# Own rows of V in four column groups, the other rows batched over eight segments

## The chip, the cores and the metric

The program runs on one core of a Trainium2 chip. The metric is the time of one execution on the device in microseconds, lower is better. One execution is profiled; its engines are called PE (TensorE, matrix products), PEld (its weight loads), DVE (VectorE), ACT (ScalarE), POOL (GpSimd) and SP (SyncE, which here only issues DMAs).

## What is computed

A transformer layer with a recurrent memory, and all its gradients. The input x has 2048 rows of 448 numbers, all in bf16. The attention goes over 64 segments of 32 rows, one after the other, with 16 heads of 256:

```
h = concat(mem, xs)                  # 8 memory rows and the 32 rows of the segment
q, k, v = h Wq, h Wk, h Wv           # 40 rows x 4096 each
p = softmax(mask(q k^T / 16))        # 40 x 40 for each head
o = (p v) Wo
mem = o[0:8]                         # memory of the next segment
out = o[8:40]
```

The layer then is `h = x + A(layernorm(x))` and `h2 = h + B(layernorm(h))`, where B is the gated network `(silu(x Wg) * (x Wu)) Wd` with 1792 hidden numbers. The kernel returns h2 and the gradients of nine inputs for a given gradient of the output. Because `mem` comes out of one segment and goes into the next, the 64 segments of the forward attention cannot run side by side, nor can those of the backward attention.

## The kernel before

Four parts follow one another: `forward_chain` (the 64 segments of the attention), `ffn_phase` (B, forward and backward), `backward_chain` (the 64 segments in reverse) and `tail_phase` (the gradients of the weights, large matrix products). Tiles lie in three arenas named arW (weights), arA and arB; PSUM has a pool of five banks `psf`, two banks `fx` and one bank `po`. A tile framework puts the instructions of each engine in order and sets the waits. What stands in `k.prio.crit()` comes first; `tc.issue_after(x)` puts an instruction behind x on x's engine. The code is unrolled.

The 40 rows of a segment are kept turned (features on partitions, `hT_roll`), the 32 rows of x in columns 0 to 31 and the memory in columns 32 to 39. The first 8 rows of x in each segment are called the rest rows here: columns 8 to 39, the other 24 rows and the memory, are the own rows. The rest rows don't depend on the recurrence. Q and K already use this: for the rest rows they are formed for eight segments at once, 64 rows in all (`rest_half`, L506), one unit of four chunks in each segment, in time for the next eight; `rest_rows` (L521) copies 8 rows of them into a segment's `qT_b` and `kT_b` on GpSimd. Units are done in segments 3 to 7 (two, two, two, one, one) for the second batch, and one in each of the segments 8 to 55. Segments 0 to 2 and 56 to 63 have none.

One segment runs like this in the program's lines:

- `qk_rows` (L590, L597): Q and K of the 32 own rows, four products of 32 columns side by side in the array; evicted, then turned by `qk_turned` (L614).
- `scores` (L698) in two halves of the heads; the mask is put into the bank first (L687). Heads come in two groups g: partitions 0 to 39 hold the queries of eight heads, partitions 64 to 103 those of the other eight.
- `shifted` and `softmax` for each half (L705 maximum, L706 subtraction, L707 exponential on ScalarE, L713 sum, L715 reciprocal, L716 product into `P_sb` in bf16).
- `value_rows` (L725) and `value_rest` (L733): V of all 40 rows, 64 stationary columns at a time (24 of them are not used), two products side by side, into four banks pV[0] to pV[3]; `value_out` evicts them into `Vs`, three on ScalarE and one on VectorE.
- `transposed_p` (L744): P turned with the identity, one matmul for each head and group (two banks `fx`), and evicted by VectorE and ScalarE into the block diagonal tile `PT_bd`.
- `values` (L757): P V for each half with 128 rows contracted, evicted into `xblk` (own rows) and `orr`.
- `out_proj` (L772), after which the sum of two halves is formed (L825 on ScalarE, L826 on VectorE). L832 turns the memory rows, L834 and L838 (GpSimd) put them into the next segment's `hT_roll`.

Behind this, each segment stores P (L843), Q and K (L845), V (L847) and the output rows (L841, L842) for later. Every 16 segments the output rows of the rest rows are formed for 16 segments at once (L876, 32 matmuls, into one `fx` bank); they are mixed into the segments that follow. The evictions all have the line of one helper: L75 on VectorE, L76 on ScalarE.

`backward_chain` reads P, Q, K and V back: `load_p` and `load_qk` (L1220, L1224), `load_v`.

## Time and profile before

| | us |
|---|---|
| median of 3 runs | 2878.65 (2863.39 to 2879.43) |
| profiled execution, its time | 2871.71 |
| profiled execution, its span | 2869.9 |
| forward chain, first L590 to the last L826 | 42.5 to 942.9 |
| one segment in the middle of it (L590 at 425.97 to L590 at 439.37) | 13.40 |
| busy in that segment: PE, DVE, ACT, POOL | 13.09, 7.52, 7.00, 4.44 |

The granted clock of TensorE is 0.988 in the mean. The span is the time from the first to the last instruction in the trace. A line of the timeline gives the start, the busy time, the engine, the line, the operation, what it writes and reads, and how often; a matmul's busy time overlaps that of the next, so the distance between starts says more about it than its length. In the chain of waits each piece has its start, its length, and what was worked on or waited for.

### The profile page before, as it was taken

The page shows a single profiled execution, that of the slowest core. Times are in us where ns is not written, and L with a number is a line of the kernel's source. Part 1 is how long each engine was busy: PE and PEld are TensorE (multiplying, and loading weights), DVE is VectorE, ACT ScalarE, POOL GpSimd, SP SyncE. Part 2 cuts the span into 40 slices and gives each one's busy share as a digit, 9 for nine tenths or more (in the row PEclk, how much of TensorE's full clock was granted, in tenths as well). Part 3 has the DMA queues.
Part 4 walks back from the last instruction along what each step waited for, and adds up shares of the span by engine and source line. Part 5 has one row for each costly group of instructions (what it writes and reads, how often), then busy time and mean ns, then how long its engine had stood idle before and what let it go on. Part 6 is the DMA issues. An engine that isn't in the chain of part 4 may idle for free.

```text
span 2869.9 us, 98023 instructions
## 1 busy us (share of the span) xinstructions
PE 2727.5 (95%) x41651; PEld 1575.5 (55%) x41651; DVE 1308.1 (46%) x3352; ACT 1046.2 (36%) x2579; POOL 929.0 (32%) x2065
## 2 busy tenths in 40 slices
PE   5999999999999999989999999999999989999998
PEld 3565555556555666645555555555655444445444
DVE  4555556465555677745555555555553111111110
ACT  2554455455454554433333433333332010111110
POOL 1222232232222232423454445545543211121211
PEclk9999999999999999989999999999999999999999
DMA  8577767777868999996777777777778998969951
GB/s 263 148 188 199 198 185 194 197 192 190 214 177 207 305 220 237 236 289 144 172 184 173 185 167 185 183 174 183 184 169 249 339 244 178 216 165 235 196 154 49
DMA packets 781806, 571.55 MB, mean 199 GB/s; under 512 B 632432, under 2 KB 673688, under 8 KB 778808
## 3 DMA queue, kind: packets, MB, share of 16 engines
q1 hardware_dynamic: 717080, 406.86, 60.7%
q0 software_dynamic: 64288, 158.41, 17.4%
q8 instruction: 328, 5.37, 0.8%
q14 instruction: 110, 0.90, 0.1%
HBM read 181.58 MB, written 244.92 MB: 149 GB/s over the span
## 4 chain that ended last, share of the span: by engine, by line
PE 73%; DMA 10%; issue 8%; ACT 3%; DVE 3%; POOL 2%; SPq 1%; POOLq 0%; ACTq 0%; DVEq 0%
PE bank L1334 9%; PE psf L1684 8%; PE psf L590 6%; PE psf L988 5%; PE psf L725 4%; PE bank L1181 4%; PE po L772 4%; PE fx L1684 3%; PE bank L1299 2%; PE fx L1113 2%; PE psf L614 2%; DMA arA<-VG 2%; PE bank L1354 2%; PE bank L1440 2%; PE psf L506 1%
## 5 line engine op out<-in xcount | busy, mean ns | idle before, releaser
L75 DVE CAST arA<-psf 128x512 bf16<-128x512 f32 (+2 forms) x285 | 159.9, 561 | 486.9 <-PE psf L1684 249.9
L76 ACT CAST arA<-psf 128x512 bf16<-128x512 f32 (+3 forms) x379 | 189.7, 509 | 523.9 <-PE psf L1684 215.2
L1334 PE MATMUL bank<-arW,arA 128*32 128x448 bf16 x6144 | 320.7, 357 | 4.9 <-DMA arW<-Tq 4.5
L76 ACT CAST arA<-bank 128x96 bf16<-128x96 f32 (+4 forms) x608 | 193.4, 376 | 111.7 <-PE bank L1322 95.5
L1684 PEld LDWEIGHTS <-arA 128*128 128x128 bf16 x1440 | 139.5, 99 | 161.9 <-issue 7.1
L1334 PEld LDWEIGHTS <-arA 128*32 128x32 bf16 x6144 | 155.8, 97 | 125.9 <-ACT arA L76 12.1
L1684 PE MATMUL psf<-arW,arA 128*128 128x512 bf16 x882 | 224.0, 383 | 0.0
L725 PE MATMUL psf<-arW,arA 128*64 128x512 bf16 x1536 | 212.2, 382 | 0.0
L590 PE MATMUL psf<-arW,arA 128*32 128x512 bf16 x3072 | 189.8, 381 | 7.8 <-DVE arA L75 0.9
L988 PE MATMUL psf<-arW 128*128 128x256 bf16 (+1 forms) x1288 | 146.1, 274 | 1.6 <-ACT arW L76 1.6
L1761 POOL DMA_DIRECT2D out_dram<-arA x96 | 51.9, 542 | 263.2 <-DVE arA L75 234.9
L1211 POOL DMA_DIRECT2D arA<-P_all x256 | 127.6, 504 | 23.1 <-issue 20.5
L75 DVE CAST arA<-bank 128x256 bf16<-128x256 f32 (+4 forms) x386 | 129.6, 391 | 6.4 <-PE bank L1181 4.1
L988 PEld LDWEIGHTS <-arW 128*128 128x128 bf16 (+1 forms) x1344 | 102.2, 97 | 51.6 <-issue 40.9
L772 PE MATMUL po<-arW,arA 128*32 128x256 bf16 (+1 forms) x4096 | 128.3, 262 | 1.7 <-DVE arA L75 1.2
L1181 PE MATMUL bank<-arW,arA 112*32 112x512 bf16 x2048 | 128.1, 392 | 1.6 <-DVE arA L1550 1.6
L590 PEld LDWEIGHTS <-arA 128*32 128x32 bf16 x3072 | 70.3, 96 | 105.2 <-issue 28.5
L1724 PE MATMUL psf<-arW 128*128 128x448 bf16 x525 | 112.8, 356 | 7.1 <-DVE arA L75 7.1
L772 PEld LDWEIGHTS <-arA 128*32 128x32 bf16 x4096 | 104.6, 96 | 9.6 <-DVE arA L75 1.5
L76 ACT CAST arB<-psf 128x64 bf16<-128x64 f32 (+1 forms) x192 | 65.1, 341 | 98.6 <-PE psf L597 76.3
L1227 POOL COPY arB<-arB 40x320 bf16<-40x320 bf16 x128 | 63.8, 498 | 114.7 <-DMA arB<-P_all 79.8
L725 PEld LDWEIGHTS <-arA 128*64 128x64 bf16 x1536 | 68.4, 109 | 52.8 <-issue 26.3
(321 smaller groups left out, 5101.0 us busy)
## 6 DMA issues: line engine op xcount, KB each, us to landing
arW<-T SPq DMA_DIRECT2D x256, 128.0 KB
X_o<-arA SPq DMA_DIRECT2D x37, 512.0 KB
T<-arA SPq DMA_DIRECT2D x64, 256.0 KB
X_v<-arA POOLq DMA_DIRECT2D x30, 512.0 KB
X_k<-arA POOLq DMA_DIRECT2D x30, 512.0 KB
X_q<-arA POOLq DMA_DIRECT2D x30, 512.0 KB
out_dram<-arA POOLq DMA_DIRECT2D x84, 128.0 KB
VG<-arA SPq DMA_DIRECT2D x64, 160.0 KB
```

Source lines behind the costliest of these rows:

```text
L75: return nc.vector.tensor_copy(out=out, in_=in_)
L76: return nc.scalar.copy(out=out, in_=in_)
L590: nc.tensor.matmul(banks[b][w][32 * q:32 * q + 32, :], lhsT=hT_roll[:, kc, sl, M:L], rhs=(Wq_sb, Wk_sb)[w][:, kc, col(q, b)], start=(b == ...
L725: nc.tensor.matmul(pV[b][64 * g:64 * g + 64, 0:512], lhsT=hT_flat[:, kc, sl * L:sl * L + 64], rhs=Wv_sb[:, kc, n * 512:(n + 1) * 512], sta ...
L772: last = nc.tensor.matmul(pO[32 * q:32 * q + 32, 0:w], lhsT=xblk[:, j, r * SEG:(r + 1) * SEG], rhs=Wo_sb[:, cj(j), 256 * dh:256 * dh + w], ...
L988: nc.tensor.matmul(ps[fp][:, f2 * 256:(f2 + 1) * 256], lhsT=Wt[lo:hi, kc, c * P:(c + 1) * P], rhs=xT[lo:hi, kc, :], start=(kc == 0 and f2 ...
L1181: last = nc.tensor.matmul(bank[32 * q:32 * q + 32, :], lhsT=lhs(c), rhs=WoT_sb[0:DQ, c, n0:n0 + 512], start=(c == 0), stop=(c == 3), skip_ ...
L1211: nc.gpsimd.dma_start(out=P4[32 * q:32 * q + 32, 2 * x + g], in_=pa[64 * g + M:64 * g + L, x])
L1227: pool_op = nc.gpsimd.tensor_copy(out=P_bd[64 * g:64 * g + L, :, g, :], in_=P_sb[64 * g:64 * g + L, :, :])
L1334: last = nc.tensor.matmul(ps[32 * q:32 * q + 32, 0:D], lhsT=lhs(j), rhs=WT[:, cj(j), :], start=(start and i < 4), stop=(stop and i >= len( ...
L1684: k.last_mm = nc.tensor.matmul(pa[i][:, 0:w], lhsT=lhs_of(b)[:, i // 2 * P:(i // 2 + 1) * P], rhs=rhs_of(q, b, i % 2), start=(b == 0), sto ...
L1724: k.last_mm = nc.tensor.matmul(pa[i][:, 0:D], lhsT=lhs_of(b, i), rhs=rhs_of(b), start=(bi == 0), stop=(bi == m + 3))
```

## The change

Only the attention is changed, mostly in `forward_chain`:

- V of the own 32 rows is formed as Q and K are: `own_wholes` and `own_halves`, 32 stationary columns, four products side by side, into two banks instead of four. Each bank is evicted in two halves of 64 partitions.
- V of the rest rows is formed for eight segments at once (`rest_v`), one unit of 256 columns by the same list of units, evicted by ScalarE and stored in a new DRAM tensor `VR`. `load_vr` loads 16 rows of it into partitions 64 to 79 of the next segment's `Vs`. The first batch is formed in segment 0. `VG`, which the backward chain reads, gets its rest rows from `VR` once in eight segments.
- The keys are put in another order: own rows first (0 to 31), rest rows last (32 to 39). Mask, `kT_b`, and in `backward_chain` the loads of K and the places of the K and V gradients follow.
- P is written twice by the softmax, once for each group, times a mask `gm` that is 1 on the group's partitions and 0 elsewhere (`P_two`: two products of 256 and 64 elements a partition for each half). Then one matmul for each head turns both groups at once into the block diagonal form; its result is evicted in one piece, the first half by ScalarE, the second by VectorE. `P_sb` for the backward chain is now formed by GpSimd, in one buffer instead of two.
- `values` contracts 80 rows instead of 128.
- The first half of a batch unit of Q and K (`rest_half` with w = 0) stands ahead of the turn of P; before it stood behind the first half of `values`.

```diff
     def rest_rows(s):
...
-        for dst, src in ((qT_b[s % 2], R[0]), (kT_b[s % 2], R[1])):
+        for dst, src, k0 in ((qT_b[s % 2], R[0], 0), (kT_b[s % 2], R[1], SEG)):
...
+    def rest_v(m, u, dst, eng):
+        bank = k.ps1()
+        for kc in range(KC):
+            for g in range(2):
+                n, c0 = 4 * g + u // 2, 256 * (u % 2)
+                rhs = Wv_sb[:, kc, n * 512 + c0:n * 512 + c0 + 256] if kc < 3 else Wv3[:, n // 2 * 512 + c0:n // 2 * 512 + c0 + 256]
+                nc.tensor.matmul(bank[64 * g:64 * g + 64, 0:256], lhsT=hR_b[m % 2][:, kc if kc < 3 else 3 + n % 2, :], rhs=rhs,
+                                 start=(kc == 0), stop=(kc == KC - 1), skip_group_check=True)
+        return k.evac(dst, bank[:, 0:256], eng)
+
+    def load_vr(s):
+        m, w = divmod(s, 8)
+        for g in range(2):
+            r0 = 64 * g + M * w
+            src = V0[r0:r0 + M, :] if s == 0 else dr["VR"][m][r0:r0 + M, :]
+            nc.gpsimd.dma_start(out=V_b[s % 2][64 + M * g:64 + M * g + M, :], in_=src)
...
                 rs = smal.tile([P, HB], FP32, name="rs")
                 nc.vector.reciprocal(out=rs[:], in_=ssum[:])
-                return nc.vector.tensor_tensor(out=P_sb[:, HB * b:HB * b + HB, :], in0=Sx,
-                                               in1=rs[:].unsqueeze(2).to_broadcast([P, HB, L]), op=ALU.mult)
+                rsm = rsm_b[b]
+                nc.vector.tensor_tensor(out=rsm, in0=rs[:].unsqueeze(2).to_broadcast([P, HB, 2]),
+                                        in1=gm.unsqueeze(1).to_broadcast([P, HB, 2]), op=ALU.mult)
+                for o, k0, n in ((0, 0, SEG), (2 * SEG, SEG, M)):
+                    to_p = nc.vector.tensor_tensor(out=P_two[b][:, :, o:o + 2 * n].rearrange("p h (g n) -> p h g n", g=2),
+                                                   in0=Sx[:, :, k0:k0 + n].unsqueeze(2).to_broadcast([P, HB, 2, n]),
+                                                   in1=rsm.unsqueeze(3).to_broadcast([P, HB, 2, n]), op=ALU.mult)
+                nc.gpsimd.tensor_tensor(out=P_sb[:, HB * b:HB * b + HB, :], in0=Sx,
+                                        in1=rs[:].unsqueeze(2).to_broadcast([P, HB, L]), op=ALU.mult)
+                return to_p
+
+            def own_wholes(b):
                 for kc in range(KC - 1):
-                    for g in range(2):
-                        n = 4 * g + b
-                        nc.tensor.matmul(pV[b][64 * g:64 * g + 64, 0:512], lhsT=hT_flat[:, kc, sl * L:sl * L + 64],
-                                         rhs=Wv_sb[:, kc, n * 512:(n + 1) * 512],
-                                         start=(b < 2 and kc == 0), stop=(b > 1 and kc == KC - 2), skip_group_check=True)
...
+                    for q in range(4):
+                        n = 4 * (q % 2) + 2 * (q // 2) + b
+                        last = nc.tensor.matmul(pV[b][32 * q:32 * q + 32, :], lhsT=hT_roll[:, kc, sl, M:L],
+                                                rhs=Wv_sb[:, kc, n * 512:(n + 1) * 512],
+                                                start=(b == 0 and kc == 0), stop=(b == 1 and kc == KC - 2), skip_group_check=True)
+                return last
+
+            def own_halves():
+                for q in range(4):
+                    m = 2 * (q % 2) + q // 2
+                    for b in range(2):
+                        nc.tensor.matmul(pV[b][32 * q:32 * q + 32, :], lhsT=hT_roll[64 * b:64 * b + 64, KC - 1, sl, M:L],
+                                         rhs=Wv3[64 * b:64 * b + 64, m * 512:(m + 1) * 512], start=(b == 1), stop=(b == 0),
+                                         skip_group_check=True)
+
+            def value_out(b, x, eng):
+                c0 = (2 * x + b) * 512
+                k.evac(Vs[0:64, c0:c0 + 512], pV[b][64 * x:64 * x + 64, :], eng)
+
+            def transposed_p(b, eng):
+                pPT = k.fx1()
                 for h in range(HB):
...
+                    nc.tensor.matmul(pPT[0:2 * L, 2 * h * L:2 * (h + 1) * L], lhsT=P_two[b][:, h, :], rhs=two,
+                                     start=True, stop=True, skip_group_check=True)
+                return k.evac(PT_bd[0:2 * L, HB * b:HB * b + HB].rearrange("p h g n -> p (h g n)"), pPT[0:2 * L, 0:2 * HB * L], eng)
...
+            if s == 0:
+                for u in range(8):
+                    rest_v(0, u, V0[:, 256 * u:256 * u + 256], "vs"[u % 2])
+                load_vr(0)
+                nc.sync.dma_start(out=dr["VR"][0], in_=V0)
...
             pS0 = scores(0, pS[0])
-            pV[0] = k.ps1()
+            pV = [k.ps1(), k.ps1()]
             with tc.issue_after(pe_at[0].ins):
-                value_rows(0)
+                own_wholes(0)
             pS1 = scores(1, pS[1])
             Sx0, _ = shifted(0, pS0)
             Sx1, sub = shifted(1, pS1)
             softmax(0, Sx0, sub)
-            p_in = softmax(1, Sx1, sub)
-            for b in range(1, 4):
-                pV[b] = k.ps1()
-            value_rows(1)
-            value_rest(0)
-            value_rest(2)
-            value_out(0, "s")
-            value_out(1, "s")
-            value_rows(2)
-            turned = transposed_p(0)
-            with tc.issue_after(turned[1].ins):
-                value_out(2, "s")
-            value_rows(3)
-            with tc.issue_after(turned[0].ins):
-                value_out(3, "v")
+            softmax(1, Sx1, sub)
+            own_halves()
+            value_out(0, 0, "s")
+            own_wholes(1)
+            value_out(1, 0, "s")
+            vr = []
+            for u in units:
+                buf = vr_b[u % 2 if bm == 0 else 0]
+                rest_v(bm + 1, u, buf, "s")
+                vr.append((u, buf))
+            rest = {u: k.ps1() for u in units[0:1]}
+            for u in rest:
+                rest_half(bm + 1, u, 0, rest[u])
+            turned = transposed_p(0, "s")
             if end:
                 k.fl.at(1)
-            transposed_p(1)
-            units = ({3: (0, 1), 4: (2, 3), 5: (4, 5), 6: (6,), 7: (7,)}.get(bu, ()) if bm == 0 else (bu,)) if bm < NSEG // 8 - 1 else ()
+            with tc.issue_after(turned.ins):
+                value_out(0, 1, "s")
+            turned = transposed_p(1, "v")
+            with tc.issue_after(turned.ins):
+                value_out(1, 1, "v")
             pv = values(0)
-            rest = {u: k.ps1() for u in units[0:1]}
-            for u in rest:
-                with tc.issue_after(pv.ins):
-                    rest_half(bm + 1, u, 0, rest[u])
             values(1)
             projected = out_proj(0, MC)
...
+        for u, buf in vr:
+            nc.gpsimd.dma_start(out=dr["VR"][bm + 1][:, 256 * u:256 * u + 256], in_=buf)
+        if bu == 3:
+            for g in range(2):
+                nc.gpsimd.dma_start(out=dr["VG"][s - 3:s + 5, L * g + SEG:L * g + L, :],
+                                    in_=dr["VR"][bm][64 * g:64 * g + 64].rearrange("(w m) n -> w m n", m=M))
...
         for g in range(2):
-            v_out = nc.sync.dma_start(out=dr["VG"][s, L * g:L * g + L], in_=Vs[64 * g:64 * g + L, :])
+            v_out = nc.sync.dma_start(out=dr["VG"][s, L * g:L * g + SEG], in_=Vs[32 * g:32 * g + 32, :])
         if not end:
             rest_rows(s + 1)
+            load_vr(s + 1)
```

## The prediction

> **What bounds the kernel now.** I read the page first: its span, the line of the engines, and the chain that ended last.
>
> ```profile
> span 2869.9 us, 98023 instructions
> PE 2727.5 (95%) x41651; PEld 1575.5 (55%) x41651; DVE 1308.1 (46%) x3352; ACT 1046.2 (36%) x2579; POOL 929.0 (32%) x2065
> PE 73%; DMA 10%; issue 8%; ACT 3%; DVE 3%; POOL 2%; SPq 1%; POOLq 0%; ACTq 0%; DVEq 0%
> ```
>
> TensorE looks like the bound, but the share is a mean over stages. The change sits in the forward chain, which by the start times of its lines runs from 42.5 to about 943 us. Its 64 segments form a recurrence. The starts of L826, one a segment, are 13.4 us apart in 42 of 63 intervals, 15.3 to 16.8 us in 15 (three groups of five, where L876 is mixed in), and 14.2 to 17.8 us in the first six. The eight last segments have none of the L506 batch work, and they still take 13.4 us. So a plain segment is not set by the amount of TensorE work; a chain of waits sets it. The chain of waits within one segment (start, length, what) shows where it leaves TensorE:
>
> ```profile
> 431.57 0.20 PE fx L698 x16
> 431.77 0.66 PE psf L725 x6
> 432.43 0.56 PE psf L733 x8
> 432.98 0.77 PE psf L725 x6
> 433.75 0.16 PE fx L744 x8
> 433.95 0.04 issue
> 433.99 0.29 ACT arB L76
> 434.30 0.59 ACT arW L76
> 434.91 0.29 ACT arB L76
> 435.19 0.03 issue
> 435.22 0.38 ACT arA L76
> 435.60 0.03 issue
> 435.63 0.45 PE psf L757 x8
> 436.07 1.86 PE po L772 x49
> ```
>
> After the second scores (L698) TensorE fills the softmax with V (L725, L733), turns P (L744), and from 433.99 four ScalarE evictions lead to the second values (L757). The VectorE rows of the same stretch in the timeline (start, busy time) are the ones that I price the new softmax by:
>
> ```profile
> 432.20 0.32 DVE L706 TENSOR_TENSOR S_sb<-fx,mx 128x160 f32<-128x160 f32 x1
> 432.44 0.31 DVE L713 TENSOR_REDUCE ssum<-S_sb 128x4 f32<-128x160 f32 x1
> 432.78 0.18 DVE L715 RECIPROCAL rs<-ssum 128x4 f32<-128x4 f32 x1
> 432.92 0.32 DVE L713 TENSOR_REDUCE ssum<-S_sb 128x4 f32<-128x160 f32 x1
> 433.16 0.38 DVE L716 TENSOR_TENSOR arB<-S_sb,rs 128x160 bf16<-128x160 f32 x1
> 433.45 0.17 DVE L715 RECIPROCAL rs<-ssum 128x4 f32<-128x4 f32 x1
> 433.65 0.32 DVE L716 TENSOR_TENSOR arB<-S_sb,rs 128x160 bf16<-128x160 f32 x1
> ```
>
> A step that needs the step before it starts 0.34 us after a 160-element reduction and 0.20 after a tiny reciprocal; one that does not need it starts 0.24 and 0.14 after. The last product ends at 433.97.
>
> **TensorE work, part by part.** In the timeline 6 matmuls of L725 (two side by side) start 0.65 us before the next line of the same shape, so one wave of 512 columns is 0.217. L590 has 24 matmuls, four side by side, in 1.41 us: six waves plus 0.11. I read 0.1 us as the price of each change of tile shape. Before, V costs 24 L725 in 12 waves (2.60), 8 L733 in two waves (0.43) and three such changes: 3.3 us. After: own rows of L725's kind need 24 matmuls in six waves (1.30), the halves one wave (0.22), rest V 8 matmuls of 256 columns in four half waves (0.44), with five changes: 2.5 us. So 0.8 us less work. The four matmuls a half that now turn P have no row: 16 of L744 take 0.12 + 0.19; the nearest, L757 with 80 moving columns, gives 0.036 each, and L832, the slowest short one, 0.11. Eight cost 0.3 to 0.9; I take 0.3 (L757 is nearest), no gain.
>
> Where does this work lie? Own V of the first half stands between the two scores, three waves as before, but the shape changes before and after it: the second scores come 0.19 late. After them stand the halves, own V, rest V and L506's first half: 0.31 + 0.75 + 0.54 + 0.57, to about 433.95 on this segment's clock. Then TensorE waits for P. All of its saving lies under that wait.
>
> **The softmax chain, which I think decides.** The second maximum starts at 431.84 + 0.19 = 432.02, its subtraction at 432.38, so the second exponential ends at 432.38 + 0.36 + 0.34 = 433.08. On VectorE, with the starts-apart above: sum 432.62, reciprocal 432.96, second sum 433.10, new small product for the mask 433.34 (priced as L715, 8 elements), second reciprocal 433.48. Then each half writes P twice in two products instead of one. L716 has 160 elements in 0.324 us; at the slope between the 256- and 512-element copies (0.41 and 0.69, about 1.05 ns an element) 256 elements cost 0.42 and 64 cost 0.22. First half: 433.62 and 433.96, ready at 434.18. Second half: mask product 434.10, products 434.30 and 434.64, ready at **434.86, 0.89 later** than before.
>
> From there, the second turn ends about 435.20, its eviction (the 40x320 VectorE eviction elsewhere takes 482 ns) starts at 435.24. The last eviction of V is ordered behind it on the same engine: 435.65 to 436.34 (0.69). Then come the last values and, also behind it on VectorE, the eviction of the first values (0.42, to 436.68), without which the output projection cannot start. So L772 starts at about 436.72 against 436.00: **+0.72 us a segment**. Everything after that hangs on L772 (L825, L832, L834) and moves along. ScalarE is not late there: first turn evicted by 434.98 (40x320 takes 420 ns), next V eviction by 435.5.
>
> At one place the Trainium skill speaks against the change. The row: the four evictions of V cost 0.59 on ScalarE and 0.69 on VectorE, whatever TensorE does in 2.5 or 3.3 us. "TensorEngine Tiling (Array Packing)", section "PSUM Bottleneck", says that packing speeds TensorE but not the eviction, which can then become the bound. The trace agrees in kind: four evictions already stand in the chain. By a count of TensorE alone the sum would be a gain of 0.8 us a segment; by this rule it would be none.
>
> **GpSimd and DMA.** P for the backward pass is now formed on GpSimd: two products a segment. No row has a two-input product there. Its 128x256 copy L855 takes 0.40, and the longest such copy, L1227 with 320 elements, 0.50 in the mean and 1.3 at worst; 0.3 to 1.3 each, I take 0.5. One store and two loads of V rest a segment are three issues like L843's 0.55. Together 2.7 us in a segment in which GpSimd is busy 4.4 of 13.4 us: hidden. What would lose the cover is L838, which the next halves (L597) need 1.05 us after it starts (426.33 to 427.38); two issues ahead of it would cost 0.1 to 0.6. The one new wait on its queue is at a batch's edge: the next segment's load of V rest waits until the eighth store has landed; behind it stand the copies L854 and L855 and, later, L838. The store can go out after 434.1 and L838 comes 5 us later, so I price it at nothing; if it took longer, it would be seven times the excess. On SP's queue the V stores (L847) only shrink from 40 rows to 32. The VectorE product L716 runs from 302 to 765 ns, median 324, and the one at 433.16, under a GpSimd copy, took 0.38; with four products now under GpSimd's, I add 0.1 us (between 0, no overlap, and 0.4). Freed second buffers (P, and the double fx bank of the turn) cost nothing while the P store (L843, issued at 434.28) has a whole segment. The reordered keys only change offsets: zero in the backward pass.
>
> **Sum.** 42 plain segments at +0.8 (0.72 + 0.1, rounded) are +34. In the 15 mixed segments L876 holds one fx bank and the old turn wanted two, so it ran in four pieces there; the new one wants one. I set their gain against the same delay: 0, between -12 and +12. The first six, with two batch units and statistics: +0.5 each, +3. Eight units of rest V ahead of the first scores: 8 x 0.44 = +3. Sum **+40 us** on the profiled execution's own 2871.7 (span 2869.9 and 1.8 around it), so 2912. That execution lies 7 us under the median of the three runs, 2878.65; I forecast **2914**, nearer to the execution that was priced.
>
> **Rivals.**
> (a) *TensorE sets the pace.* For it: 95% busy, and the chain is 73% TensorE. Then the new softmax must be ready by 434.2, when TensorE comes to the second turn, 0.7 before my sum, and V's last eviction must not stand in the way. A segment would lose the 0.8 of V and some 0.1 of the old wait: 42 x -0.9 - 15 x 0.5 + 6 = -40: 2832. Against it: the eight segments without batch work are no shorter. Chance 0.18.
> (b) *Nearly even.* The rows overlap better (the shorter product starts sooner, or the values' eviction goes ahead of V's on VectorE): +0.3 on plain segments, and the mixed segments keep 0.8 for the single bank: 42 x 0.3 - 12 + 6 = +7: 2879. Chance 0.24.
> (c) *Worse, by queues.* The first V eviction is ready at 432.36 (the halves start at 431.91, an L733 lasts 0.40, ScalarE follows 0.05 later) and goes ahead of the second exponential on ScalarE (+0.2), GpSimd's products stretch VectorE's (+0.3): 42 x 1.3 + 15 x 0.5 + 6 = +68: 2940. It decides from the moment that V's halves end before the second subtraction does, which by my clock they do. Chance 0.16.
> My forecast has 0.42. That the batch does not do what it says (rest V loaded too late) I hold for unlikely: V's rows are wanted 9 us into a segment and can be loaded a segment ahead.
>
> **How the numbers follow.** Within 1%, 29 us, is about what a measurement of this kernel can tell from no change. The forecast's own range, +0.45 to +1.1 a plain segment, is 42 x 0.45 + 6 = 25 to 42 x 1.1 + 6 = 52, so 2897 to 2924; a quarter of its chance falls within 1%. Faster: all of (a), 0.18. Same: (b) 0.24 and 0.10 of the forecast. Slower: the rest, 0.48. For 8 in 10 I go down into (a), to 2842, for half of its chance, and up to 2952, past (c).
>
> **What would show it.** After, a plain segment of 14.0 to 14.4 us between L826's successors; TensorE idle before the second turn, released by VectorE; V's work near 2.5 us; the last V eviction on VectorE in the chain ahead of the output projection; GpSimd busy about 7 us a segment. The forecast is wrong if plain segments are under 13.4 us, or if the time changes outside the forward chain.

## The result, and the profile after

The change made the kernel **slower by 5.3%**: ratio 1.0531, 95% interval 1.0486 to 1.0576 (median 3025.95 us against 2875.72 on the same chip, four runs each). The forecast was slower, by 1.4%; the time lies outside its range (2842 to 2952 us).

The profiled execution took 3027.65 us. Its page, in the lines that answer to those shown of before, with TensorE's granted clock over 40 slices of the span as the third:

```profile
span 3025.9 us, 98770 instructions
PE 2778.1 (92%) x41651; PEld 1610.4 (53%) x41651; DVE 1380.3 (46%) x3549; ACT 1057.7 (35%) x2575; POOL 1096.0 (36%) x2395
PEclk8999999998998899999999999999999999999999
PE 68%; DMA 11%; DVE 9%; issue 8%; POOL 1%; ACT 1%; SPq 1%; DVEq 0%; POOLq 0%; ACTq 0%
```

VectorE's share of the chain has gone from 3 to 9%, and TensorE, with less work to do, is busy for longer (2778.1 us against 2727.5). The spans differ by 156.0 us. By the starts of L862 (L826 before) all of it lies in the forward chain: 7.9 us up to the first of these additions, 148.9 from the first to the last (1035.7 against 886.8), and 0.8 less behind them. Of the 148.9, the 42 plain segments have 125.6, the 15 mixed ones 12.1, the first six 11.2.

The waits of TensorE in the forward chain (us in total, times, longest) name one place above all, the turn of P; before, the old turn (L744) waited 2.0 us for VectorE in all:

```profile
PE fx L777 <- DVE om L746: 33.6, 45, 0.9
PE fx L777 <- DVE arB L746: 25.5, 35, 2.8
```

The timeline of one plain segment (start, us, engine, line), whose Q and K begin at 442.87 and which lasts 14.91 us (L746 are VectorE's products into P, L749 GpSimd's, L777 is the turn of P, L804 the output projection, L75 VectorE's evictions):

```profile
450.29 0.45 POOL L749 TENSOR_TENSOR arB<-S_sb,rs 128x160 bf16<-128x160 f32 x1 [3.73 <-ACT S_sb L733]
...
450.50 0.66 DVE L746 TENSOR_TENSOR arB<-S_sb,om 128x256 bf16<-128x256 f32 x2
...
451.39 0.45 POOL L749 TENSOR_TENSOR arB<-S_sb,rs 128x160 bf16<-128x160 f32 x1 [0.65 <-DVE rs L741]
451.48 0.78 DVE L746 TENSOR_TENSOR om<-S_sb,om 128x256 bf16<-128x256 f32 x2
...
452.31 0.35 PE L777 MATMUL fx<-ident,om 128*80 128x80 bf16 x4 [0.76 <-DVE om L746]
...
452.69 0.49 DVE L75 CAST arB<-fx 80x320 bf16<-80x320 f32 x1 [0.44 <-PE fx L777]
...
453.21 1.15 DVE L75 CAST arA<-psf 64x512 bf16<-64x512 f32 x2
...
454.41 0.43 PE L804 MATMUL po<-arW,arA 128*32 128x256 bf16 x10
```

This is the forecast's chain, step by step, and longer. Both pairs of products run under a GpSimd product and take 0.66 and 0.78. The turn follows the second pair, its eviction follows the turn, and the line at 453.21 is the last eviction of V and, behind it, that of the first values. The output projection starts 11.54 us into the segment, against 10.03 before and 10.75 forecast.

But most segments take longer still, 16 to 17 us. Here is the second thing, in a table of stretches of the same trace (from:to, length, busy us of PE, PEld, DVE, ACT and POOL with the number of instructions, granted clock, DMA share, GB/s), cut where the granted clock can change:

```profile
465.74:469.15 3.41, 1.85 (x34) 1.27 (x30) 2.84 (x9) 1.65 (x5) 0.45 (x1) 1.00 0.00 0
469.15:472.56 3.41, 3.27 (x65) 2.67 (x64) 0.70 (x4) 0.49 (x2) 0.00 (x0) 0.50 0.57 153
...
482.80:486.21 3.41, 1.86 (x38) 1.39 (x38) 2.84 (x9) 1.89 (x6) 2.71 (x9) 1.00 0.17 50
486.21:489.63 3.42, 3.40 (x66) 2.75 (x68) 0.95 (x4) 0.49 (x2) 1.52 (x4) 0.50 0.71 207
```

TensorE is busy for 1.85 of 3.41 us while the softmax runs, and in the next 3.41 us its clock is granted at 0.50. The output projection falls into that stretch: its 64 matmuls take 3.49 us instead of 1.93. In the forward chain 162.9 us are granted at half clock, 48 stretches that begin in 41 of 63 segments (the expectation of experiment 1 says 47 segments); before, it was one stretch of 3.4 us.

### The profile page after: what moved, and what is told of

Read it like the earlier page. It is cut to its first block, busy times and chain, and to the rows that moved or that the text cites. A ratio compares the mean times of both kernels' runs of the same rounds, so it can differ in the third digit from the quotient of the medians.

```text
span 3025.9 us, 98770 instructions
## 1 busy us (share of the span) xinstructions
PE 2778.1 (92%) x41651; PEld 1610.4 (53%) x41651; DVE 1380.3 (46%) x3549; ACT 1057.7 (35%) x2575; POOL 1096.0 (36%) x2395
## 4 chain that ended last, share of the span: by engine, by line
PE 68%; DMA 11%; DVE 9%; issue 8%; POOL 1%; ACT 1%; SPq 1%; DVEq 0%; POOLq 0%; ACTq 0%
PE bank L1377 9%; PE psf L1728 7%; PE po L804 6%; PE psf L618 6%; PE psf L1031 5%; DMA arA<-VG 4%; PE bank L1224 4%; PE psf L642 2%; PE fx L1728 2%; PE bank L1342 2%; PE fx L1156 2%; PE bank L1397 2%; PE bank L1483 2%; PE psf L757 2%; DVE arB L746 1%
## 5 line engine op out<-in xcount | busy, mean ns | idle before, releaser
L76 ACT CAST arA<-psf 128x512 bf16<-128x512 f32 (+4 forms) x383 | 193.6, 506 | 592.2 <-PE psf L1728 215.2
L75 DVE CAST arA<-psf 128x256 bf16<-128x256 f32 (+3 forms) x289 | 161.9, 561 | 469.6 <-PE psf L1728 249.9
L1377 PEld LDWEIGHTS <-arA 128*32 128x32 bf16 x6144 | 156.0, 97 | 127.8 <-issue 13.3
L618 PE MATMUL psf<-arW,arA 128*32 128x512 bf16 x3072 | 195.9, 388 | 7.0
L804 PE MATMUL po<-arW,arA 128*32 128x256 bf16 (+1 forms) x4096 | 184.2, 333 | 6.8
L804 PEld LDWEIGHTS <-arA 128*32 128x32 bf16 x4096 | 140.6, 117 | 34.6 <-DVE arA L75 16.2
L75 DVE CAST arA<-bank 128x256 bf16<-128x256 f32 (+4 forms) x386 | 129.5, 390 | 6.3 <-PE bank L1342 3.8
L618 PEld LDWEIGHTS <-arA 128*32 128x32 bf16 x3072 | 71.1, 97 | 108.3 <-issue 34.1
L517 PE MATMUL psf<-arA,arW 128*128 128x64 bf16 x2048 | 87.2, 202 | 24.2 <-DMA arW<-in_A_Wq_dram 10.1
L862 DVE TENSOR_TENSOR arB<-po,om 64x256 bf16<-64x256 f32 x64 | 27.3, 426 | 178.2 <-ACT om L861 178.0
L757 PE MATMUL psf<-arW,arA 128*32 128x512 bf16 x1536 | 106.4, 383 | 0.0
```

What stands on the lines that cost most here:

```text
L75: return nc.vector.tensor_copy(out=out, in_=in_)
L76: return nc.scalar.copy(out=out, in_=in_)
L517: last = nc.tensor.matmul(bank[:, w * 256 + i * 64:w * 256 + (i + 1) * 64], lhsT=lhsT, rhs=hR_b[m % 2][:, kc if kc < 3 else 3 + w, :], sta ...
L618: nc.tensor.matmul(banks[b][w][32 * q:32 * q + 32, :], lhsT=hT_roll[:, kc, sl, M:L], rhs=(Wq_sb, Wk_sb)[w][:, kc, col(q, b)], start=(b == ...
L757: last = nc.tensor.matmul(pV[b][32 * q:32 * q + 32, :], lhsT=hT_roll[:, kc, sl, M:L], rhs=Wv_sb[:, kc, n * 512:(n + 1) * 512], start=(b == ...
L804: last = nc.tensor.matmul(pO[32 * q:32 * q + 32, 0:w], lhsT=xblk[:, j, r * SEG:(r + 1) * SEG], rhs=Wo_sb[:, cj(j), 256 * dh:256 * dh + w], ...
```

## Experiments

**Theory:** two causes, one feeding the other. VectorE's chain from the scores to the first values is 1.5 us longer, and the idle time that it leaves on TensorE makes the clock drop. **Rivals:** V itself, its batched rows and their trips through memory; products that are dear by their operands, without GpSimd; a clock that drops for reasons of its own. In this table a plain segment is the commonest length without half clock, the forward chain goes from the first L826 or its successor to the last, and the half clock is its time in that chain, all by the profiled execution. In the changed kernel one plain segment is left without half clock when they are counted from addition to addition; from Q and K to Q and K there are eight, of 14.90 us. The edits below are shown in short: dots and plain words stand for code that is left out.

| kernel | ratio to before (95%) | plain segment | forward chain | half clock |
|---|---|---|---|---|
| before | 1 | 13.39 | 886.8 | 3.4 |
| changed | 1.0531 (1.0486 to 1.0576) | 15.0 | 1035.7 | 162.9 |
| warm | 1.0399 (1.0349 to 1.0449) | 14.90 | 1001.6 | 30.7 |
| no_pool | 1.0437 (1.0385 to 1.0488) | 14.51 | 1009.8 | 143.4 |
| v_alone | 1.0066 (1.0034 to 1.0098) | 13.76 | 912.7 | 21.2 |
| p_alone | 1.0221 (1.0169 to 1.0273) | 14.61 | 950.0 | 0.0 |
| before_late3 | 1.0053 (1.0028 to 1.0077) | 13.90 | 909.2 | 6.8 |
| before_late5 | 1.0571 (1.0537 to 1.0604) | 15.1 | 1046.6 | 166.9 |
| late_pool | 1.0401 (1.0368 to 1.0434) | 14.50 | 997.4 | 130.3 |
| late_evict | 1.0158 (1.0122 to 1.0194) | 13.70 | 919.8 | 24.0 |
| mended | 1.0062 (1.0035 to 1.0089) | 13.47 | 895.7 | 20.5 |
| mended_sp | 0.9999 (0.9977 to 1.0020) | 13.47 | 883.0 | 17.4 |
| mended_split | 1.0017 (0.9997 to 1.0037) | 13.47 | 883.7 | 17.1 |
| v_mended | 1.0074 (1.0050 to 1.0098) | 13.85 | 904.9 | 13.7 |

**1. TensorE kept busy (warm).**

```
 def transposed_p(b, eng):
     pPT = k.fx1()
+    if b == 1:
+        fill(pPT, 3, last_tp[0])   # 3 matmuls ident x Wv, 512 columns
...
 po = k.ps1()
+if b == 1:
+    fill(po, 2, last)
```

> The changed kernel with matmuls added that do no work: three of 512 columns ahead of the second turn of P, and two ahead of each of the two banks of the second values, seven a segment, in banks that the real matmuls overwrite. In the changed kernel 47 of 63 segments have a stretch of 3.41 us in which TensorE's granted clock is 0.5, 162.9 us in all in the forward chain, against 3.4 us before. Theory (two parts: a VectorE chain that is 1.5 us a segment longer, and a clock that is halved because TensorE idles under that chain): the stretches at half clock go, segments come at 15.0 to 15.3 us, the time falls by 60 to 80 us to about 2945 to 2965 us, and the forward chain stays some 70 to 90 us longer than before. Rival (the halved clock has nothing to do with the idle time, or is an answer to load): the stretches stay, or get more, and the time is the same or up to 30 us longer, as the added matmuls cost 0.2 to 0.5 us a segment.

More work for TensorE, less time: 2989.36 us. Plain segments take 14.90 us, two of 42 with half clock in them. The time is above the range for a reason in the experiment: the last segment takes 34.63 us, because its added matmuls read weights that the next stage is just loading over (TensorE stands 17.0 us ahead of them). Without those 19.7 us the chain is 982 us, 54 below the changed kernel's. That much is the clock; the other 95 of the 148.9 are there with only 10 us at half clock left outside the last segment.

**2. Without GpSimd's products (no_pool).** L749 is taken out.

> The changed kernel without the two products on GpSimd; the P that the backward stage reads is zero, so the gradients are not the reference's. Theory (GpSimd's product, running beside them, stretches VectorE's products): the 256-element product falls from 0.53 and 0.60 us to 0.42, the 64-element one from 0.21 and 0.29 to 0.2, the second turn starts 0.4 us earlier, and the time falls by 25 us or more, more if the halved clock gets rarer with it. Rival (the products are dear by their operands, read with two stride-zero axes, and GpSimd has no part): the four products keep their durations within 0.05 us and the time stays within 10 us.

The products by shape (the last three columns are busy us, mean ns of one, and us idle before), first with GpSimd's products beside them, in the changed kernel:

```profile
L746 DVE TENSOR_TENSOR om<-S_sb,om 128x256 bf16<-128x256 f32 x60 | 36.4, 607 | 2.0
L746 DVE TENSOR_TENSOR arB<-S_sb,om 128x256 bf16<-128x256 f32 x61 | 31.9, 523 | 0.0
```

and without:

```profile
L747 DVE TENSOR_TENSOR arB<-S_sb,om 128x256 bf16<-128x256 f32 x62 | 27.0, 435 | 0.0
L747 DVE TENSOR_TENSOR om<-S_sb,om 128x256 bf16<-128x256 f32 x62 | 26.3, 425 | 2.0
```

Contention, then, and not the operands: 0.18 and 0.09 us on one product each, and 0.39 on a plain segment (14.90, as warm has it, to 14.51). The time falls by 25 us to 3000.64; the half clock stays.

**3. V alone, and P alone (v_alone, p_alone).** v_alone takes `own_wholes`, `own_halves`, `rest_v` and the two banks of the change with the old product and the old turn; p_alone takes the old V with the new products, key order and turn.

> V as in the changed kernel, P as before: one product a half on VectorE, two banks, one matmul a head and group, the values contracted over 128 rows. The order of P's keys does not fit V's rows, so the attention output is not the reference's. Theory (all of the loss lies in P's products and in the clock that falls with the idle time under them): segments at 13.4 us or up to 0.5 below, TensorE still waiting for the second turn, the forward chain within 30 us of the kernel before, 2840 to 2895 us. Rival (V itself, its batched rows, their trips through memory and the wait for them carry the loss): 2960 us or more, with segments over 14.5 us.

> V as before, in four banks of 64 columns, nothing batched; P as in the changed kernel, with the four products on VectorE, the two on GpSimd, the eight matmuls of the turn and values over 80 rows, which do not fit V's rows, so the attention output is not the reference's. Theory: it carries the chain of VectorE: segments 0.8 to 1.6 us over 13.4 where V's longer TensorE work does not cover it, few stretches at half clock since TensorE has more to do, 2925 to 2980 us. Rival (V carries the loss): within 25 us of the kernel before.

Both times lie in their ranges, but V alone has longer segments where equal or shorter ones were expected. P carries most: +1.22 a plain segment, V +0.37; together 1.59, and both at once cost 1.51 (14.90). P alone sees no half clock, with TensorE idle 1.08 us a segment, because the old V gives it more to do. V alone is no gain although TensorE has 0.9 us less work for V in a segment: its idle time there (the gaps between its matmuls in a plain segment) goes from 0.29 to 1.03 us. Its 0.37 goes with the batch unit, which the change put ahead of the turn: the last five segments, which have no unit, take 13.4 to 13.5 us, nearly as before (13.39), and there the first turn starts 8.54 us behind the addition, as before, and not 9.10. In the changed kernel the wait for P covers the unit (in warm 14.90 with one, 14.89 without), so it is in part chance that the two costs add up to nearly the whole.

**4. The delay without the change (before_late5, before_late3).**

TensorE's order is held as it was by `issue_after`, not shown here.

```
-return nc.vector.tensor_tensor(out=P_sb[...], in0=Sx, in1=rs..., op=ALU.mult)
+for _ in range(1 + more):     # more = 5 or 3 in the second half
+    to_p = nc.vector.tensor_tensor(out=P_sb[...], in0=Sx, in1=rs..., op=ALU.mult)
+return to_p
```

> The kernel before, with the last product of P (VectorE, 0.32 us) done six times over instead of once, same values, and TensorE's order held as it was. Nothing of the change is in it and TensorE's work is untouched; only the second turn of P comes five products, some 1.7 us, later. In the four kernels seen so far, on the grid of 3.41 us in which the granted clock changes, each stretch with TensorE busy for under 0.60 of it was followed by one at half clock, and none with over 0.65 was. Theory (the clock is halved by TensorE's own idle share in a stretch, whatever made it idle): plain segments without half clock at 14.9 to 15.2 us, half clock in at least half of the segments, segments with it at 16 us or more, forward chain longer by 110 to 170 us, 2985 to 3045 us in all. Rival (the half clock comes from something in the change, its shapes, its batched rows or its trips through memory): no more than 10 us at half clock in the forward chain, all plain segments at 15.0 us, 2960 to 2985 us.

Confirmed, with nothing of the change in the kernel. It was as slow as the changed kernel, and its table of stretches reads the same (columns as above):

```profile
453.66:457.07 3.41, 1.58 (x41) 0.96 (x37) 2.94 (x10) 1.41 (x5) 0.52 (x1) 1.00 0.14 49
457.07:460.48 3.41, 3.41 (x75) 3.01 (x73) 0.91 (x4) 0.92 (x4) 0.44 (x2) 0.50 0.68 237
```

The evictions of the first turned P and of V came to stand among the added products, so P was ready 2.4 us later rather than 1.7.

> The kernel before with the last product of P done four times instead of once, the smaller dose of the same delay; TensorE's order held, its work untouched. With two products more (five) the second turned P came 2.4 us later, TensorE idled 1.97 us a segment and plain segments took 15.1 us, or 16.7 where a stretch at half clock fell into them. Theory (the clock has a threshold in TensorE's busy share of a stretch of 3.41 us, near 0.6): the idle time is 1.1 to 1.5 us, so the share stays above 0.6 in nearly all stretches, plain segments take 14.3 to 14.7 us, under 30 us at half clock, 2915 to 2945 us. Rival (the clock gives way in proportion to the idle time): 80 to 110 us at half clock, 2955 us or more.

The size was missed: the delay came out at 0.5 us a segment and TensorE's idle time at 0.79, below the 1.1 expected, so the time is below the range too. The question is answered all the same. Per segment the small dose costs 0.51 us and no clock; the large one costs 1.7 us without and 3.3 with the half clock. In proportion to the idle time 0.79 us would have brought 67 us at half clock (166.9 x 0.79 / 1.97); it was 6.8.

**5. The repairs (late_pool, late_evict, mended).** Each adds one to the one before. On the chip of these runs and of before_late5 the kernel before took 2865.70 us, against 2875.48 in experiments 1 to 3, so the ratios compare better than the times.

```
 late_pool:  GpSimd forms P as P_two[.., o:o+n] + P_two[.., o+n:o+2n],
             second half first, so not before VectorE's last product
 late_evict:
+            v01 = value_out(0, 1, "s")
             turned = transposed_p(0, "s")
-            value_out(0, 1, "s"), then transposed_p(1, "v")
-            value_out(1, 1, "v")
+            value_out(1, 1, "s")
+            transposed_p(1, "v")
 mended:     pS1 = scores(1, pS[1])  ahead of  own_wholes(0)
```

> The changed kernel with GpSimd's part moved out of the way: P for the backward stage is the sum of the two masked halves of the turned P, which GpSimd adds once VectorE has done all four products. Theory (GpSimd's product stretches VectorE's only while they run together, and the evictions behind them do not mind): VectorE's products at 0.41 to 0.43 and 0.22 us, plain segments without half clock at 14.5 us, half clock still there, 2990 to 3010 us, as in the kernel without GpSimd's products. Rival (GpSimd's work costs wherever it runs, since what it collides with next are the evictions of the turned P, or the copies behind it): evictions longer by 0.1 us or more each, segments at 14.9 us, 3010 to 3030 us.

Segments at 14.50, products at 0.42 to 0.43: as without GpSimd's products. The evictions behind them, nearly all of which now run beside GpSimd's sums, did not change (0.486 and 0.692). The time, 2979.47 us, is 11 under the range.

> As the kernel with GpSimd's part late, and the last two evictions of V on ScalarE, the first of them ahead of the eviction of the first turned P, the second behind it; VectorE then goes from the second turned P straight to the values. Theory (the eviction of V on VectorE, 0.69 us between the second turned P and the first values, sets the chain): the output projection starts 0.5 to 0.7 us earlier, plain segments at 13.8 to 14.0 us, TensorE idle about 1 us a segment, so hardly any half clock (under 30 us), 2900 to 2935 us. Rival (ScalarE now holds the values back by as much): within 15 us of the kernel with GpSimd's part late.

The timeline of VectorE behind the second turn, with the values now directly behind P:

```profile
505.64 0.49 DVE L75 CAST arB<-fx 80x320 bf16<-80x320 f32 x1 [0.44 <-PE fx L775]
506.05 0.41 DVE L75 CAST arA<-psf 128x256 bf16<-128x256 f32 x1
```

0.41 us apart, where the changed kernel had V's eviction between and 1.2. A plain segment is 0.80 shorter, more than the 0.69 of the eviction itself, and with TensorE's idle time at 0.97 us the half clock goes from 130 to 24 us. The ratio fell by 2.4 points for one eviction moved to ScalarE and another put ahead of the turn.

> As the kernel with ScalarE's evictions, and the second half of the scores right behind the first, V's first bank behind both. Theory: the second maximum starts 0.2 us earlier, as in the kernel before, plain segments at 13.6 to 13.8 us, no half clock after the first segments, 2885 to 2920 us: most of the loss gone, still not faster than before. Rival (V's first bank, now later, holds its evictions and then the values back): no better than the kernel with the late evictions, 2900 us or more.

A little better than expected, 2884.16 us, of which the chip has a part: the second maximum starts 6.53 us behind the addition that ends a segment, against 7.00 in late_evict and 6.79 in the kernel before, and a plain segment takes 13.47.

**6. Loads of V's rest rows on SP's queue (mended_sp).**

```
-nc.gpsimd.dma_start(out=V_b[s % 2][...], in_=src)
+nc.sync.dma_start(out=V_b[s % 2][...], in_=src)
```

> The mended kernel with the loads of the batched V rows on SP's queue instead of GpSimd's. In the mended kernel plain segments take 13.47 us, but three segments lose 2.1 to 5.9 us: GpSimd stands in front of such a load (3.4 us for the rows to land in memory) with the copy of the next segment's memory rows behind it, and TensorE waits for that copy. Theory (the wait on GpSimd's queue costs the time): the load no longer holds that copy, the long segments at each eighth one go, the time falls by 5 to 15 us to 2870 to 2880 us. Rival (the loads hold something on SP instead, or the long segments come from elsewhere): 2880 us or more.

In the mended kernel the waits of GpSimd had this line, and those of TensorE in the segment at 848 to 868 us the next:

```profile
POOL arA L537 <- DMA VR<-S_sb: 17.7, 6, 4.2
```

```profile
PE psf L625 <- POOL arA L878: 3.6, 1, 3.6
```

The load at each batch's edge waits for the store of V's rest rows to land, on a queue where the copy for the next Q and K stands behind it; and a stall of 3.6 us costs the clock as well. On SP's queue the load is gone from GpSimd's waits. The forward chain is 12.7 us shorter, but not all of it was this wait. Of the segments at a batch's edge one gives back 4.9 us, one 1.3 and the others nothing; 5.8 us come from a segment at 326 us, in which GpSimd stood 3.6 us ahead of another load (L696), with the same copy behind it. The time is that of the kernel before, 0.9999 (0.9977 to 1.0020). This is the best version found: level, not faster.

Level is a mean of two kinds of segment, though. With a batch unit a plain segment takes 13.47 us; the last ones, without a unit, mostly take 13.13, against 13.39 before. P is ready at the same time in both (9.35 and 9.34 us behind the addition). With a unit (L517) TensorE goes from it straight to the first turn (L775); without one it waits there for P:

```profile
636.88 0.64 PE L517 MATMUL psf<-arA,arW 128*128 128x64 bf16 x16
637.35 0.33 PE L775 MATMUL fx<-ident,arB 128*80 128x80 bf16 x4
...
900.13 0.83 PE L755 MATMUL psf<-arW,arA 128*32 128x512 bf16 x12
901.37 0.34 PE L775 MATMUL fx<-ident,arB 128*80 128x80 bf16 x4 [0.41 <-DVE arB L746]
```

So here the unit ahead of the turn holds back the segments that have one: their first turn starts at 9.28 us, and at 8.73 without. The unit behind the values again, as before the change, was not tried with the repairs.

**7. Two that gained nothing (mended_split, v_mended).** The first replaces the reciprocal and the mask product by two reciprocals of 64 partitions, the second gives the new V with the old P the same repairs.

> As the mended kernel with the loads on SP's queue, and the reciprocal and the mask product replaced by two reciprocals of 64 partitions each, which write the masked layout straight (the other columns stay zero); four VectorE instructions a segment as before, but none waits for the one ahead of it. Theory: P is ready 0.1 to 0.3 us earlier, plain segments take 13.2 to 13.4 us, 2860 to 2875 us, level with the kernel before or just under it. Rival (TensorE now sets the pace, or the second exponential does): plain segments at 13.4 us or more, no gain over the kernel with the loads on SP's queue.

The outcome is the rival's, 13.47 us again, but the theory was not put to the test: P is not earlier but 0.16 us later. VectorE's last product starts 9.30 us behind the addition, against 9.13 in mended_sp, because both reciprocals of the first half now stand ahead of the second sum (7.86 against 7.61). That delay tells something all the same: segments without a unit become 0.17 us longer by it (13.30 against 13.13), those with one do not, so P does not set their time.

> The kernel with V as in the change and P as before, with the same three repairs (last two evictions of V on ScalarE, second scores behind the first, loads on SP's queue); its keys do not fit V's rows, so the attention output is not the reference's. Theory (V's four column groups take 0.8 us of TensorE's work away, which pays once the evictions are off VectorE's chain): plain segments at 12.8 to 13.2 us against 13.39 before, 2835 to 2865 us, faster than the kernel before. Rival (the chain of VectorE and ScalarE takes as long as before whatever TensorE does): plain segments at 13.4 us, 2865 us or more.

Missed, 13.85 us. P is ready 8.6 us behind the addition, 0.3 earlier than before. But TensorE waits 0.46 us ahead of the second turn and 0.24 ahead of the values, both times for an eviction of P on ScalarE, which has all four evictions of V now:

```profile
PE fx L767 <- ACT arB L76: 22.9, 49, 0.6
PE psf L780 <- ACT arB L76: 11.9, 49, 0.3
```

So the chain moved from VectorE to ScalarE in part; without a unit a segment takes 13.50 us, so 0.35 of the 0.46 over the kernel before go with the unit. V's shorter work with the old P did not shorten a segment in either order tried. Whether another order would was not tried.

## Why the prediction was wrong in size

**What bounds the kernel: right.** A plain segment was set by a chain and not by the amount of TensorE work; the last five segments of v_alone show it, with less TensorE work than before and none of the time saved. Once the chain was mended the order of TensorE's work did count (experiment 6). "Time changes outside the forward chain" did not happen (0.8 us).

**TensorE's work: right.** V was priced at 3.3 to 2.5 us; what its matmuls add to TensorE's busy time in four plain segments is 3.31 before and 2.42 with the change (in mended_sp, at full clock). The turn's eight matmuls add 0.31 in the commonest segment of mended_sp, where others follow them at once (0.3 priced); with TensorE waiting around them, as in the segment shown, they take 0.34 and 0.35. TensorE's arrival at the first turn, "to about 433.95", leaves out the 0.19 by which the forecast had just moved the second scores: by its own rows it is about 434.13, still ahead of P. The second scores are 0.21 late (0.19). And all the saving was lost under the wait, as the forecast said. The rule of the Trainium skill, "TensorEngine Tiling (Array Packing)", section "PSUM Bottleneck", that packed columns do not help the eviction, holds here: the eviction moved by late_evict was worth 0.80 us a segment, the 0.9 us of TensorE work nothing.

**The softmax chain: right in its steps, small in nearly all.** In the segment shown, by its offsets from the first Q and K matmul: second maximum 6.09 us (6.05 forecast), P ready 9.38 (8.89), eviction of the turned P 9.82 (9.27), V's eviction 10.34 (9.68), output projection 11.54 (10.75). So 0.79 was missing. The prices of the products were right (0.42 and 0.22; 0.43 and 0.22 measured without GpSimd), and so was the order. Of this 0.49 lies ahead of P, of which GpSimd has 0.39, and 0.30 behind it: 0.06 from P to the eviction of the turned P, 0.11 in that eviction, 0.13 in the two behind it. I had taken each of these from an instruction's busy time or a nearest row, and each took somewhat more from start to start. The sum had 0.1 for GpSimd beside this clock, so a plain segment at full clock was 0.7 short: +0.8 forecast, +1.5 measured.

**The step that failed first: the overlap with GpSimd**, "I add 0.1 us (between 0, no overlap, and 0.4)". It was 0.39, the end of its range; the value taken in the middle came from a copy beside a product, while what runs here is two inputs from SBUF on both engines. The Trainium skill, "SBUF — State Buffer", section "SBUF: two separate sides", says that VectorE with two SBUF inputs and GpSimd share a port pair that the first takes for its whole instruction. The trace agrees, in both directions. In the 94 products of 256 elements that started 0.24 to 0.48 us before GpSimd's ended, VectorE's ended 0.28 us behind GpSimd's each time, so it took 0.52, 0.64 or 0.76 us, against 0.43 undisturbed; it is as if all of it but the first 0.15 us had waited. In the 13 where VectorE's was ahead, it took its 0.41, and GpSimd's ended 0.31 us behind it, 0.51 to 0.71 long against 0.45. VectorE's evictions from PSUM beside GpSimd do not stretch (late_pool).

**The step that failed most: there was no term for the clock.** The range was built from durations at full clock. Of the 148.9 us, 54 are the half clock as experiment 1 measures it; part of the 7.9 ahead of the first addition may be too (17.1 us at half clock there, none before). These 54 alone are more than the whole forecast, +40. The profile of before showed the clock at 0.988 and one half-clock window, and I read nothing from it.

**Mixed segments: 0 forecast, between -12 and +12; measured +12.1.** Without half clock they are still +11 (warm), so the single bank for the turn saved nothing that the chain did not take. With the chain mended they do gain: 14 us less than before in mended_sp. The first six were +11.2 (+3 forecast), three of them with half clock.

**The rivals.** (c), worse by queues, 2940 us, was nearest, and both of its mechanisms are there: V's first eviction starts ahead of the second exponential (7.34 and 7.82 us behind the addition in warm, which makes the exponential 0.1 later, 0.2 priced) and GpSimd stretches the products (0.39, 0.3 priced). (a), TensorE setting the pace, was refuted: in warm a segment without a batch unit takes as long as one with it (14.89 and 14.90). (b) was off by the same chain. The wait of GpSimd on the store at a batch's edge, priced "at nothing", costs some 6 us in the mended kernel (4.9 and 1.3, experiment 6), not because the store is slow, 4.2 us at most, but because L878 stands right behind it.

## What to carry to other kernels

When a change moves work from the engine that looks busy onto a chain that it waits for, price the chain from start to start, and ask what each engine's new instruction will run beside. Then add up the idle time that the busy engine is left with in any 3.4 us: here a delay that left TensorE idle for up to 1.1 us a segment cost itself, and at 1.5 to 2.0 us it cost nearly double through the clock (by the mean of the plain segments, 1.1 became 2.2 in late_pool and 1.7 became 3.1 in before_late5). Order around the last wait (which eviction goes first, on which engine) was worth 2.4% and needed no less work.

## What the runs showed of the hardware

**The granted clock follows TensorE's busy share in fixed stretches of 3.413 us.** In the traces of all fourteen kernels I cut the forward chain, from the ninth segment to the eighth from the end, on the grid on which the granted clock changes, and took each stretch at full clock with TensorE's busy share and the clock of the next one:

| busy share | stretches | next one at half clock |
|---|---|---|
| under 0.50 | 49 | 49 |
| 0.50 to 0.60 | 60 | 53 |
| 0.60 to 0.65 | 17 | 6 |
| 0.65 and more | 2686 | 1 |

The share is from modelled ends of matmuls, so the border is blurred. The "each" in the expectation of before_late5 was too strong: seven of 60 stretches between 0.50 and 0.60 had full clock behind them. A grid step at half clock was followed by full clock in 107 of 114 cases. In the changed kernel the commonest distance from one to the next is 17.07 us (five grid steps, 22 of 47), since a segment with half clock in it lasts almost as long. The idle time need not be in one piece: in 29 of the 30 stretches of the changed kernel that half clock followed, no gap between matmuls in it exceeded 0.9 us. The Trainium skill, "TensorE: Matmul & The Clock Gate", section "HAM oscillation — how this bites in real kernels", gives the rule as no idle gap over some 3.4 us; the window length agrees with these traces, the rule as a bound does not, since gaps of under 0.9 us that add up to some 1.4 to 1.6 in one window were enough. Its section on a second failure mode tells of short idle gaps that do it, without a number; the table above is one for this kernel.

**Added matmuls that do nothing can shorten a kernel.** Seven a segment cost no time that could be seen, and took some 54 us off the chain, the last segment aside.
